# Attention in front of a soft mixture of experts: scores by single heads into two banks, masks added on TensorE, and a written order for four engines

## The chip, the cores and the metric

The kernel runs on one core of a Trainium2 chip. A core has engines that work side by side, each through its own queue in order: TensorE (PE, matrix products and transposes, into the eight banks of PSUM), VectorE (DVE), ScalarE (ACT), GpSimd (POOL, which here works on SBUF only) and SyncE (SP, which issues the transfers). The metric is the device time of one execution in microseconds; a lower time is better. The profile is of one execution; its times are microseconds from the start of its span.

## The reference

There are 8 batches, 8 heads of 64 columns, 512 local and 32 global tokens. A global query sees all 544 keys. A local query sees the 32 global keys and the local keys at a distance of at most 32. The output of the attention is the input `x` of a soft mixture of 8 experts with 4 slots each.

```python
s_ll = scale * np.matmul(q_l, k_l.transpose(0, 1, 3, 2))
mask = np.abs(pos[:, None] - pos[None, :]) <= window          # 32
s_ll = np.where(mask, s_ll, -1000000000.0)
a_l = sm(np.concatenate([s_lg, s_ll], axis=-1))
out_l = np.matmul(a_l, np.concatenate([v_g, v_l], axis=2))
...
logits = x @ phi                       # 4352 tokens, 32 slots
d = softmax(logits, over the tokens)   # dispatch
slot_input = d.T @ x
slot_out[e] = np.maximum(slot_input[e] @ w1[e], 0.0) @ w2[e]
return softmax(logits, over the slots) @ slot_out             # combine
```

## The kernel before

**Units.** A unit is one batch and four heads, two pairs; there are 16. The 512 local queries of a head are 16 blocks of 32. A block needs 128 keys: its own, the block before, the block after, and the global one. The host lays the keys out so that these 128 are contiguous or nearly so (the global block is repeated after every third block).

**Scores** (`scores`, line 159). The queries lie block-diagonally: two heads share 128 rows, and 64 columns of weights hold the block's 32 queries of either head, zeros elsewhere. One product gives 64 rows of scores over 128 keys, so a PSUM bank (128 rows by 512) holds four blocks of all four heads. A unit has four such banks (`kb`). The trace shows each fp32 product as two matmuls with their weight loads.

**Softmax.** DVE adds the masks to the bank (line 166), takes the maximum of each group of 128 (line 177) and subtracts it into SBUF, turning the order of the keys where needed (line 183). PE transposes the result (line 200), and ACT takes the exponential on the way out of the bank (line 204). `pv` (line 220) multiplies with the values, which carry a column of ones for the denominator; blocks use one of three forms of the values, the loaded one and two copies shifted by 32 rows that `make_v` writes: `va` on POOL (lines 143, 144), `vb` on ACT (lines 147, 148). DVE divides (lines 229 to 231).

**Global queries.** Products of 480 and 64 columns (lines 241, 246), two maxima on DVE (lines 249, 250), four shifts on ACT (line 259), five transposes (line 268), 20 products (line 278), four scaled copies on ACT (line 286).

**Dispatch** (`moe_steps`). When a batch is complete, its 512 tokens are transposed (`xt`, line 313, copied out on ACT at line 316), multiplied with `phi` (line 323), go through a running softmax over the tokens (lines 346 to 368), the weights are turned (`turn`, lines 382 to 391; `turn_logits` puts the logits into the same bank, line 397, copied on ACT at line 399), and the slots' sums are updated (line 406, added at line 413). The global tokens are dispatched in two halves of four batches.

**Experts.** After the attention come the first product (line 564), hidden layer, second product (line 738), and the combination (line 767). Weights come in 64 pages of 512 KB, of which 30 have room of their own and the others take buffers that the attention gives back.

**PSUM.** Three banks for scores (`psS`), two for transposes (`psT`), two for values (`psV`) and one for the dispatch (`psM`).

**Order.** In the attention a planner puts the instructions of each engine in order by its own costs. From the last unit's end on, PE follows an order written out by hand (`manual_schedule`), and within the last softmax DVE and ACT too. `pieces` cuts a batch's dispatch into five steps that are run between the banks of the next units.

## Time and profile before

| what | value |
|---|---|
| time, median of 3 (lowest to highest) | 324.7 us (324.51 to 325.45) |
| span of the profiled execution | 324.0 us |
| PE busy | 294.7 us, 91% |
| DVE busy | 220.3 us, 68% |
| ACT busy | 186.7 us, 58% |
| POOL busy | 48.6 us, 15% |
| moved by DMA | 76.26 MB, mean 235 GB/s |

The profiled execution has no time of its own beside its span; the span is 0.7 us under the median of the timed runs. In the rows, `L159` is line 159 of the kernel, `s<-k,qlo` says that a product writes tile `s` from `k` and `qlo`, and `x16` counts instructions. PEld is the loading of weights, which overlaps the products. A row of the chain of waits has the start, the time that the piece holds the chain, and what it is. A row of the groups has the busy time, the mean nanoseconds of one instruction, and the idle time ahead with what ended it.

### The profile page before, as it was taken

How to read it: one execution, taken by the hardware profiler on the slowest of the kernel's cores; microseconds unless marked ns; L12 is line 12 of the kernel's file. 1: busy time of each engine (PE TensorE's matmuls, PEld its weight loads, DVE VectorE, ACT ScalarE, POOL GpSimd, SP SyncE). 2: the span in 40 equal slices, each digit the busy share in tenths (PEclk: the TensorE clock that was granted, in tenths of full speed). 3: DMA queues.
4: the chain of work that ended last, by engine and by line, in shares of the span. 5: the costliest groups of instructions: out<-in, count | busy, mean ns of one | idle time of the engine just before them, and what ended most of it. 6: DMA issues, size and time to landing. Idle time of an engine off the chain costs nothing.

```text
span 324.0 us, 12624 instructions
## 1 busy us (share of the span) xinstructions
PE 294.7 (91%) x5277; PEld 217.9 (67%) x5277; DVE 220.3 (68%) x730; ACT 186.7 (58%) x538; POOL 48.6 (15%) x72
## 2 busy tenths in 40 slices
PE   6789999999999999999999999999999999999600
PEld 5677877777777877777678778777876433665500
DVE  1877868696788677875886786868785795244600
ACT  1368577586847675767476756848584320263600
POOL 2312212031111111111111120303110000000000
PEclk9999999999999999999999999999999999999955
DMA  6878787789968897755444535355548999967792
GB/s 193 258 251 246 259 269 280 239 261 293 315 231 270 284 324 246 230 170 160 137 106 160 171 87 173 96 171 149 156 165 293 405 393 406 409 238 271 239 351 61
DMA packets 30969, 76.26 MB, mean 235 GB/s; under 512 B 3136, under 2 KB 12352, under 8 KB 30912
## 3 DMA queue, kind: packets, MB, share of 16 engines
q1 hardware_dynamic: 30912, 75.45, 70.3%
q8 instruction: 42, 0.69, 0.9%
q14 instruction: 15, 0.12, 0.1%
HBM read 66.52 MB, written 8.91 MB: 233 GB/s over the span
## 4 chain that ended last, share of the span: by engine, by line
PE 81%; ACT 5%; DVE 4%; DMA 3%; issue 1%; SPq 1%; DVEq 0%; ACTq 0%
PE s L159 21%; PE o L220 11%; PE t L200 10%; PE xt L313 5%; PE po L738 5%; PE g L241 5%; PE ph L564 5%; PE tg L268 3%; PE pc L767 3%; PE pl L323 3%; PE pa L406 3%; PE og L278 2%; ACT xg L286 2%; DMA qhi<-in_qT_dram 2%; DMA v<-in_vS_dram 1%
## 5 line engine op out<-in xcount | busy, mean ns | idle before, releaser
L166 DVE TENSOR_TENSOR s<-s,con 128x64 f32<-128x64 f32 (+1 forms) x112 | 35.3, 315 | 43.5 <-PE s L159 30.2
L143 POOL COPY va<-v 128x650 f32<-128x650 f32 x32 | 23.4, 732 | 190.1 <-PE o L220 173.0
L159 PE MATMUL s<-k,qlo 128*64 128x128 f32 x512 | 47.4, 298 | 1.8 <-DMA qlo<-in_qT_dram 1.6
L183 DVE TENSOR_TENSOR sp<-s,mx 128x256 f32<-128x256 f32 (+5 forms) x128 | 48.2, 417 | 0.2
L159 PEld LDWEIGHTS s<-k,qlo 128*64 128x64 f32 x512 | 37.5, 204 | 11.3 <-issue 9.3
L220 PE MATMUL o<-v,pt 128*32 128x65 f32 x768 | 43.7, 223 | 1.5 <-ACT xg L286 1.4
L177 DVE TENSOR_REDUCE mx<-s 128x4 f32<-128x512 f32 x64 | 43.9, 687 | 0.9
L204 ACT ACTIVATE pt<-t 128x256 f32<-128x256 f32 x128 | 41.1, 383 | 4.9 <-PE t L200 4.7
L220 PE MATMUL o<-va,pt 128*32 128x65 f32 x768 | 42.2, 222 | 0.6
L147 ACT COPY vb<-v 64x260 f32<-64x260 f32 x62 | 25.2, 406 | 28.3 <-DMA v<-in_vS_dram 11.0
L159 PE MATMUL s<-k,qhi 128*64 128x128 f32 x512 | 39.4, 293 | 1.8 <-DMA qhi<-in_qT_dram 1.8
L220 PE MATMUL o<-vb,pt 128*32 128x65 f32 x512 | 40.9, 223 | 0.0
L200 PE MATMUL t<-con,sp 128*128 128x128 f32 x256 | 39.6, 284 | 0.3 <-ACT pt L204 0.2
L159 PEld LDWEIGHTS s<-k,qhi 128*64 128x64 f32 x512 | 32.9, 202 | 7.1 <-issue 6.0
L220 PEld LDWEIGHTS o<-v,pt 128*32 128x32 f32 x768 | 32.6, 110 | 6.7 <-ACT xg L286 2.8
L220 PEld LDWEIGHTS o<-va,pt 128*32 128x32 f32 x768 | 31.9, 110 | 3.9 <-PE og L278 1.2
L286 ACT ACTIVATE xg<-og,rg 32x64 f32<-32x64 f32 x64 | 19.5, 305 | 22.7 <-PE o L220 18.5
L200 PEld LDWEIGHTS t<-con,sp 128*128 128x128 f32 x256 | 27.3, 141 | 4.8 <-ACT pt L204 0.4
L220 PEld LDWEIGHTS o<-vb,pt 128*32 128x32 f32 x512 | 30.5, 110 | 0.0
L231 DVE TENSOR_TENSOR xh<-o,r 128x256 f32<-128x256 f32 x64 | 26.6, 416 | 0.8
L148 ACT COPY vb<-v 64x260 f32<-64x260 f32 x62 | 25.3, 408 | 0.8
L144 POOL COPY va<-v 32x650 f32<-32x650 f32 x32 | 23.0, 719 | 2.0
(150 smaller groups left out, 434.2 us busy)
## 6 DMA issues: line engine op xcount, KB each, us to landing
w<-in_w_dram SPq DMA_DIRECT2D x64, 512.0 KB, 6.8
v<-in_vS_dram SPq DMA_DIRECT2D x32, 390.0 KB, 3.9
k<-in_kT_dram SPq DMA_DIRECT2D x15, 672.0 KB, 6.6
out_dram<-ob SPq DMA_DIRECT2D x16, 512.0 KB, 5.2
qhi<-in_qT_dram SPq DMA_DIRECT2D x32, 144.0 KB, 3.7
qlo<-in_qT_dram SPq DMA_DIRECT2D x32, 128.0 KB, 3.6
k<-in_kT_dram SPq DMA_DIRECT2D x1, 512.0 KB, 4.2
out_dram<-ob SPq DMA_DIRECT2D x4, 128.0 KB
```

Source lines behind the costliest of these rows:

```text
L143: nc.gpsimd.tensor_copy(va, v[:, 0:5])
L147: copy(vb[64:128, m:m + 2], v[64:128, m:m + 2])
L148: copy(vb[0:64, m:m + 2], v[0:64, m + 1:m + 3])
L159: nc.tensor.matmul(ps[64 * pr:64 * pr + 64, i, :], q[:, :, q0 + i, pr], ks[u][:, pr, s0:s0 + P], start=True, stop=True)
L166: nc.vector.tensor_add(a, a, m)
L177: nc.vector.reduce_max(mx, ps, axis=AX.X)
L183: nc.vector.tensor_tensor(sp[:, t0:t1, b0:b0 + a1 - a0], ps[:, t0:t1, a0:a1], bc(mx[:, t0:t1], a1 - a0), ALU.subtract)
L200: tlast[0] = nc.tensor.transpose(pt[:, i, :], sp[:, i, :], ident)
L204: nc.scalar.activation(e, pt[:, :, 64 * pp:64 * pp + 64], AF.Exp, scale=SCALE)
L220: ins = nc.tensor.matmul(po[32 * cc:32 * cc + 32, t2, jj, :], pts[u, kb, pp][:, i, 32 * jj:32 * jj + 32], (vs, vas, vbs)[cls][u, pp][:, m, ...
L231: nc.vector.tensor_tensor(xhs[u][:, 2 * th:2 * th + 2, P * pp:P * pp + P].rearrange("p t (h d) -> p t h d", h=2), po[:, :, :, 0:D], bc(r, ...
L286: nc.scalar.mul(xg[p0:p0 + 32, 256 * g + D * j:256 * g + D * j + D], po[32 * j:32 * j + 32, 0:D], r[32 * j:32 * j + 32])
```

## The change

- **Half-units.** A unit is worked in two halves of eight blocks (`k` counts 32 of them). The eight blocks of four heads fill one tile of two banks.
- **Scores.** Queries are laid out plainly. One product takes the 64 rows of one head and 32 query columns, over 128 keys. The heads of a pair lie in the two row halves and write different banks; pair and block choose one of four column groups. A half-unit has 32 such products, 64 matmuls in a trace. Key windows are read through strided views, so that all blocks have the same order of keys and nothing is turned.
- **Masks.** A bf16 mask of a whole bank is multiplied with a bf16 identity into each bank ahead of the scores, which accumulate onto it. The constants bring the masks as a transfer of their own (`msk`), cast at the start.
- **Softmax.** One maximum and one shift over both banks on DVE, two banks of transposes, each with one exponential.
- **Values.** One tile of two banks per half-unit, one reciprocal, two multiplications. Both shifted copies of the values are made on POOL.
- **Global queries.** Products of 512, 32 and 96 columns into a two-bank tile, one maximum, one shift on ACT. Their value products and all of the dispatch use the two `psT` banks.
- **PSUM.** Two tiles of two banks for scores and global scores (`psA`), one of two for values (`psV`), two banks `psT`; the split of before comes back after the attention.
- **Loads.** Keys, queries and values of a unit come as one transfer each, with two buffers each.
- **Order.** PE, DVE, ACT and POOL follow the written order through the attention and up to the first product.

```diff
+PAIRS = [
+    [(0, 1), (4, 7), (3, 6), (2, 5)],
+    [(10, 13), (9, 12), (8, 11), (14, 15)],
+]
...
+    psV = p_ps.enter_context(tc.tile_pool(name="psV", bufs=1, space=PS))
+    psA = p_ps.enter_context(tc.tile_pool(name="psA", bufs=2, space=PS))
...
+    def make_v(k):
...
+        nc.gpsimd.tensor_copy(va, v[:, m0:m1])
+        nc.gpsimd.tensor_copy(va[0:32], v[0:32, m0 + 1:m1 + 1])
+        nc.gpsimd.tensor_copy(vb[64:128], v[64:128, m0:m0 + 2])
+        nc.gpsimd.tensor_copy(vb[0:64], v[0:64, m0 + 1:m0 + 3])
...
+    def masks(k):
+        ps = psA.tile([P, 2, 512], F32, tag="s", name=f"s{k}")
+        for hh in range(2):
+            nc.tensor.matmul(ps[:, hh, :], identb, maskb[:, k % 2, :], start=True, stop=False, skip_group_check=True)
+        pss[k] = ps
...
+    def scores(k):
+        u, a = k // 2, k % 2
+        for s, cs in enumerate(PAIRS[a]):
             for pr in range(2):
+                for j, c in enumerate(cs):
+                    g = 2 * pr + j
+                    for hh in range(2):
+                        nc.tensor.matmul(
+                            pss[k][32 * g:32 * g + 32, hh, P * s:P * s + P],
+                            qs[u][64 * hh:64 * hh + 64, pr, 32 * c:32 * c + 32], window(u, c, hh, pr),
+                            start=False, stop=True, skip_group_check=True)
+
+    def shift(k):
+        ps = pss.pop(k).rearrange("p h (s j) -> p (h s) j", j=P)
+        mx = xp.tile([P, 8], F32, tag="mx", name=f"mx{k}", bufs=2)
+        nc.vector.tensor_reduce(mx, ps, axis=AX.X, op=ALU.max, negate=True)
+        sps[k] = a2.tile([P, 8, P], F32, tag="sp", name=f"sp{k}", bufs=2)
+        nc.vector.tensor_tensor(sps[k], ps, bc(mx, P), ALU.add)
+
+    def transpose_exp(k):
...
+        for hh in range(2):
+            pt = psT.tile([P, 4, P], F32, tag="t", name=f"t{k}_{hh}")
+            for s in range(4):
+                nc.tensor.transpose(pt[:, s, :], sp[:, 4 * hh + s, :], ident)
+            nc.scalar.activation(e[:, hh], pt, AF.Exp, scale=SCALE)
...
+    def global_scores(u):
+        k = ks[u]
+        pg = psA.tile([P, 1024], F32, tag="s", name=f"g{u}")
+        for c0, n, src in ((0, 512, 32), (512, 32, 21 * 32), (544, 96, 17 * 32)):
+            for pr in range(2):
+                nc.tensor.matmul(pg[64 * pr:64 * pr + 64, c0:c0 + n], qg[:, pr, :], k[:, pr, src:src + n],
+                                 start=True, stop=True)
+        pgs[u] = pg
+
+    def global_shift(u):
+        pg = pgs.pop(u)[:, 0:640]
         m1 = xp.tile([P, 1], F32, tag="m1", name=f"m1_{u}")
+        nc.vector.tensor_reduce(m1, pg, axis=AX.X, op=ALU.max, negate=True)
+        nc.scalar.activation(spg, pg, AF.Identity, bias=m1)
...
         def turn():
             n = R.stop - R.start
-            ptl = psM.tile([P, 2, P], F32, tag="m", name=f"ptl{name}")
+            ptl = psT.tile([P, 2, P], F32, tag="t", name=f"ptl{name}")
...
+    order = tc.manual_schedule(engines={ENG.PE, ENG.DVE, ENG.Activation, ENG.Pool})
+    order.__enter__()
+    nc.vector.tensor_copy(identb, ident)
+    nc.vector.tensor_copy(maskb, mtmp)
+    make_qg(0)
+    masks(0)
+    scores(0)
+    shift(0)
...
+    def dispatch(b, srcs, name, k0):
...
+            steps.setdefault((k0, "c"), []).append(lambda: (xt(0), xt(1)))
+            steps.setdefault((k0 + 2, "c"), []).append(lambda: (xt(2), xt(3)))
+            k0 += 2
+        steps.setdefault((k0, "b"), []).append(logit)
+        steps.setdefault((k0 + 1, "c"), []).append(lambda: turn_logits(turn()))
+        steps.setdefault((k0 + 2, "b"), []).append(slots)
+
+    for b in range(B - 1):
+        dispatch(b, xlocal(b), str(b), 4 * b + 5)
+    dispatch(None, xglobal(0), "g0", NU + 5)
...
+    for k in range(NH):
+        u = k // 2
+        if k % 2 == 0 and k >= 2:
+            global_transpose(u - 1)
+        run(k, "c")
+        if k >= 1:
+            transpose_exp(k - 1)
+        if k + 1 < NH:
+            masks(k + 1)
+        if k >= 2:
+            values(k - 2)
+        if k % 2 == 0 and k >= 2:
+            global_values(u - 1)
+        run(k, "b")
+        if k + 1 < NH:
+            if k % 2 == 1:
+                make_qg(u + 1)
+            scores(k + 1)
+            shift(k + 1)
+        if k % 2 == 0:
             global_scores(u)
+            global_shift(u)
...
+        make_v(k)
...
-    order = tc.manual_schedule(engines={mybir.EngineType.PE})
-    order.__enter__()
...
+    global_transpose(NU - 1)
+    run(k, "c")
+    transpose_exp(k - 1)
+    values(k - 2)
+    global_values(NU - 1)
...
     xt(0)
     xt(1)
+    values(k - 1)
...
     st6["sums"](pa6[0], 0)
     st6["add"](pa6[0], slice(0, 256))
     logits(0)
     logits(1)
+    xtg(0)
     xt(2)
+    xt(3, True)
+    for hc in range(4):
+        logitsg(hc)
     logits(2)
     logits(3)
```

## The prediction

> **What bounds the kernel now.** I read the page's shares first, then the chain of waits in order of time, then the groups by line and form, then the stretches.

> ```profile
> PE 294.7 (91%) x5277; PEld 217.9 (67%) x5277; DVE 220.3 (68%) x730; ACT 186.7 (58%) x538; POOL 48.6 (15%) x72
> PE   6789999999999999999999999999999999999600
> PE 81%; ACT 5%; DVE 4%; DMA 3%; issue 1%; SPq 1%; DVEq 0%; ACTq 0%
> ```

> TensorE (PE) is busy nearly throughout and makes 81% of the chain that ends last. Matmul durations overlap, so I price PE by how long a run of one kind holds the chain, with its count:

> ```profile
> 40.10 0.59 PE t L200 x4
> 40.69 1.01 PE g L241 x4
> 41.70 0.17 PE g L246 x4
> 41.87 1.02 PE t L200 x8
> ...
> 45.75 0.66 PE s L159 x8
> 46.41 1.02 PE xt L313 x8
> 47.43 0.67 PE s L159 x6
> 48.10 0.71 PE og L278 x40
> ...
> 53.33 0.57 PE pl L323 x16
> 53.90 1.13 PE s L159 x16
> 55.03 0.60 PE o L220 x32
> ...
> 59.05 1.00 PE pa L406 x16
> ...
> 70.00 1.01 PE g L241 x4
> ...
> 223.41 1.01 PE g L241 x4
> ...
> 251.32 0.31 DVE top L343
> ```

> Comparing runs of 4 and 8 transposes: each costs (1.02-0.59)/4 = 0.109 us, plus about 0.15 per run, which is paid when the kind of matmul (its tile of the array) changes. So 128 fp32 columns through one full-width tile take 109 ns. Scores, two tiles side by side: (1.13-0.66)/8 = 0.058. Values, four tiles: (0.60-0.13)/32 = 0.0146 for 65 columns. Column tiles thus run in parallel. The global scores' g rows recur every 14.6 us per unit of four heads (40.69 to 70.00 is two units), and of that little is idle: attention is bound by PE. At 251.32 the last softmax begins; the rest, up to 324.0, is expert work that the change leaves as it is.

> **The change part by part.** The fixed order makes each engine go through its work as written. A batch is four half-units k (32 in all); in each PE does: transposes of k-1, masks of k+1, values of k-2, scores of k+1; even ones add global transposes, global values and, last, the global scores of the unit; a dispatch adds four xT transposes in two odd ones, logits, turn and slot sums. PE work of such a cycle, in us:

> - probability transposes 32 x 0.109 = 3.5, as before;
> - values 256 x 0.0146 = 3.7, as before (fewer, larger divisions follow);
> - global transposes 10 x 0.109 = 1.1 and values 2 x 0.58 = 1.2; xT 16 x 0.109 = 1.7; logits 32 x 0.029 = 0.9; turn 0.2; slot sums 0.9: all as before;
> - global scores: 640 instead of 544 columns, (1.01+0.17-0.15)/544 x 640 = 1.2, twice, 2.3;
> - scores: 256 instructions of 128 columns instead of 128. Eight tiles (two row halves, four column groups) take turns. The trace has no row halves. Bounds: 0.029 us each, as logits with four column tiles (0.57-0.11)/16, if row halves take turns; 0.0146, as values, if they overlap (half of 0.029, and the shortest spacing shown). The two halves read other partitions and write other banks, so I take 0.0146: 3.7, where 128 x 0.058 = 7.4 is removed;
> - masks: eight new bf16 matmuls of 512 columns. Bounds from the nearest rows:

> ```profile
> 1.19 3.70 PE L118 MATMUL pw<-wrm 128*128 128x256 bf16 x18 [1.19 <-DVE wrm L474]
> 284.73 0.67 PE pc L767 x4
> ```

> Eighteen of 256 bf16 columns in 3.7 at the start give 0.39 for 512, the fp32r products (0.67-0.15)/4 x 2 = 0.26. I take 0.26, from warm mid-kernel work: 2.1.

> Sum 21.4. Mode runs: four in an even half-unit, three in an odd, 14 x 0.15 = 2.1. PE work 23.5 a cycle, against 29.3 measured now; the fixed order also saves the many short runs (about 30 a cycle now).

> [...]

> What the other engines lose and gain:

> ```profile
> L177 DVE TENSOR_REDUCE mx<-s 128x4 f32<-128x512 f32 x64 | 43.9, 687 | 0.9
> L183 DVE TENSOR_TENSOR sp<-s,mx 128x512 f32<-128x512 f32 x16 | 11.0, 690 | 0.2
> L183 DVE TENSOR_TENSOR sp<-s,mx 128x128 f32<-128x128 f32 x16 | 4.5, 279 | 0.0
> L249 DVE TENSOR_REDUCE m<-g 128x1 f32<-128x480 f32 x16 | 10.3, 646 | 0.1
> L259 ACT ACTIVATE spg<-g,m 128x384 f32<-128x384 f32 x16 | 9.6, 600 | 0.1
> L316 ACT COPY xT<-xt 128x512 f32<-128x512 f32 x31 | 17.0, 589 | 6.6 <-PE xt L313 6.4
> L166 DVE TENSOR_TENSOR s<-s,con 128x64 f32<-128x64 f32 (+1 forms) x112 | 35.3, 315 | 43.5 <-PE s L159 30.2
> L147 ACT COPY vb<-v 64x260 f32<-64x260 f32 x62 | 25.2, 406 | 28.3 <-DMA v<-in_vS_dram 11.0 <-issue 8.3 <-PE o L220 6.6
> L143 POOL COPY va<-v 128x650 f32<-128x650 f32 x32 | 23.4, 732 | 190.1 <-PE o L220 173.0 <-DMA v<-in_vS_dram 17.1
> L397 PE MATMUL ptlg<-con,lTg 32*128 32x32 f32 x1 | 0.2, 245 | 0.3 <-DVE dg L391 0.3
> ```

> DVE loses the mask adds, 35.3; from 690 and 279 an element costs 1.07 ns over a fixed 0.14, so a two-bank maximum and a two-bank shift are 1.24 each, 2.5 a half-unit. ACT loses the vb copies (2 x 25), which go to POOL: about 2.7 a half-unit by 732 for 650, 85 in all, behind PE's other half-units and out of the way. The larger loads have two buffers and a half-unit or more of slack. What these savings relieve was not the bound, so I price them at nothing.

> What the order costs. I walk through the four lists: each instruction starts when the one ahead of it on its engine and its last input are done. Times run from PE's end of scores k+1 (0):

> - *Odd half-units with xT.* The global scores stand last in the even one. DVE starts the shift at 0.24 (pipeline 0.17 and signal), ends at 2.75; only then the global maximum of 640 (0.82): 3.5; ACT's one global shift (640 elements, 0.28+0.53 by the 600 ns form) runs 3.6 to 4.4. Behind it on ACT stand the two xT copies. PE ends the global scores at 1.3 and the eight xT transposes at 2.3; both transpose banks are then full, and the probability transposes need the first xT copy, 4.35 to 4.95, so PE waits from 2.3 to 5.0 (2.6 before rounding). Everything of the next score bank is queued behind. Two a cycle.
> - *Even half-unit with turn.* The second transpose of the turn waits for DVE's copy d, as the last row shows. That copy now stands behind the whole shift, and the shift behind the running softmax (which waits for ACT): it ends 3.4 after 0, while PE has 1.2 of work. With 0.2 and 0.15 of bank waits before it: 2.3 there.
> - Small bank waits with two transpose banks for everything: 1.0 a cycle.

> Cycle: 23.5 + 2 x 2.6 + 2.3 + 1.0 = 32.0, against 29.3. Half-units are 8.2 (odd), 6.5 or 9.1 (even).

> **Sum**, against the profiled execution (span 324.0; the median, 324.7, is 0.7 above it):

> - *Start to the third unit's global scores,* 40.69 now:

> ```profile
> 4.58 5.73 DMA qhi<-in_qT_dram
> 23.76 4.30 DMA v<-in_vS_dram
> 0.00:10.00 10.00, 5.85 (x50) 4.46 (x50) 3.29 (x8) 1.28 (x1) 1.89 (x7) 1.00 0.77 219
> ```

>   k, q, constants and masks are 1.92 MB; at 219 GB/s 8.8 us after 0.7 of issue, and 1.0 for the two casts (1024 elements) and signals: first mask at about 11. The same walk over half-units 0 to 4, which have no dispatch, gives 25.2. 36.2, so -4.5; both waits above end inside it.
> - *Six cycles, 40.69 to 223.41,* 182.7 now: 6 x 32.0 + 3.8 for the dispatch of the first global half, with a turn wait of its own, = 195.5 (by half-units unrounded). +12.8.
> - *From there to the last softmax,* 27.9 now. Global scores 1.3, three half-units (8.2, 6.5, and 6.4 without masks and scores), then the written tail: PE work 9.3, and waits 5.7 (1.9 in the turn, 1.6 until ACT's four global copies free a bank, 1.2 until DVE has divided the last values, the rest small), 15.1: 37.5. +9.6.

> 324.0 - 4.5 + 12.8 + 9.6 + 0.7 = 342.6.

> **Rivals.**

> *The row halves take turns* (the change doesn't do what it says): scores 0.029 each, 0.93 more a half-unit, of which the waits swallow a little: +25, 368. For it: no row shows row tiles. Against it: column tiles overlap fully. [...]

> *Faster: the waits aren't there.* Place: ACT's and DVE's queues. If xT copies pass the global shift and d passes the shift, or the work is planned apart from the text as in the attention now, 15 waits of 2.6 and 8 of 2.3 go, 57 in all: 285 at full, 314 at half. It decides from 18 saved, i.e. 0.8 off each of the 23. For it: PE work falls by 5.8 a cycle, and now the same transposes and copies rarely stall. Against it: one queue per engine, the order given for all four, and the d wait stands in a row.

> *Loads late*: q and k come as whole tiles; if units 1 and 2 each wait once more as at 23.76, +9, 352.

> **How the numbers follow.** Forecast 0.50 (own range 331 to 353: 0.4 a wait either way and start +-2); row halves in turn 0.15; waits gone, in part or whole, 0.30; loads late 0.05. Under 0.3% (1 us) is what this measurement can't tell from no change. Faster is 0.27 of the third case, same 0.03, slower the rest, 0.70. The range goes from 302, which leaves out the deeper half of the third case, to 368.

> **What would show it.** PE waits of over 2 us before probability transposes in odd half-units, ended by the ACT copy of xT; one of about 2 before the second turn transpose, ended by DVE d; score runs of 64 at about 1.1 us (2.0 if halves take turns); mask matmuls at 0.22 to 0.39. Wrong if the global scores recur every 14 us or less per unit.

## The result, and the profile after

The changed kernel takes 380.44 us (median of 4 runs, 377.95 to 382.9), the kernel before 325.07 beside it: ratio 1.170, 95% interval 1.164 to 1.176. It is slower, as forecast, but by 55 us where 18 were forecast, and it lies outside the range (302 to 368). The profiled execution has a span of 380.8 us. Three of the kernels further down also had runs in a slower state; their times and ratios are of the faster runs alone.

First the page of the kernel after: the busy time of the engines, TensorE (PE) in 40 slices, the granted clock in the same slices, and the queue that brings instructions.

```profile
PE 282.1 (74%) x6398; PEld 198.7 (52%) x6429; DVE 177.9 (47%) x390; ACT 128.9 (34%) x296; POOL 94.5 (25%) x167
PE   4887587777877977766777777977796789999800
PEclk9999898889888989998896888988899899999965
q8 instruction: 50, 0.82, 0.9%
```

Every engine but POOL has less to do than before (PE 294.7, DVE 220.3, ACT 186.7), and PE is idle for a quarter of the span, where it was idle for a tenth. Two things in these lines stood in no step of the prediction: the clock is cut during attention, and PE has 12,827 recorded instructions (before 10,554), which come in 50 blocks of 16 KB (before 42).

PE's longest waits in the kernel after (what waits, for what: us in total, times, longest):

```profile
PE t L205 <- ACT xT L310: 28.4, 13, 2.4
PE ptl L390 <- DVE d L384: 12.3, 7, 2.4
PE s L187 <- issue: 7.2, 5, 3.6
PE o L224 <- issue: 5.3, 11, 1.3
...
PE og L268 <- issue: 2.9, 2, 1.9
PE xtg L302 <- ACT xT L310: 2.4, 1, 2.4
```

The first two rows are the two waits of the forecast, at their places and up to 2.4 us long (forecast 2.6 and 2.3). The three "issue" rows, 15.4 us, are time in which PE waits for nothing that the profile shows; the kernel before has one such row among its waits:

```profile
PE tg L268 <- issue: 0.9, 1, 0.9
```

The timeline around one odd half-unit with xT shows the first wait at work, and its sequel:

```profile
114.46 1.36 PE L243 MATMUL g<-k,qg 128*64 128x512 f32 x12
114.59 1.22 DVE L195 TENSOR_REDUCE mx<-s 128x8 f32<-128x1024 f32 x1
115.75 1.09 PE L308 MATMUL xt<-con,xh 128*128 128x128 f32 x8
115.84 1.22 DVE L197 TENSOR_TENSOR sp<-s,mx 128x1024 f32<-128x1024 f32 x1
116.99 0.81 DVE L250 TENSOR_REDUCE m<-g 128x1 f32<-128x640 f32 x1
117.89 0.79 ACT L251 ACTIVATE spg<-g,m 128x640 f32<-128x640 f32 x1 [2.08 <-DVE m L250]
118.58 1.06 ACT L310 COPY xT<-xt 128x512 f32<-128x512 f32 x2
119.22 1.97 PE L205 MATMUL t<-con,sp 128*128 128x128 f32 x8 [2.37 <-ACT xT L310]
```

The shift, the global maximum, the global shift and the xT copies run one behind the other, and eight transposes wait 2.37 us for them. Then these eight take 1.97 us, though eight of the same width took 1.09 at 115.75. The windows of 1 us over the same stretch say why (the number behind POOL's is the granted clock):

```profile
117.00:118.00 1.00, 0.00 (x0) 0.00 (x0) 0.80 (x2) 0.11 (x1) 0.00 (x0) 1.00 0.73 239
...
119.00:120.00 1.00, 0.78 (x4) 0.79 (x5) 0.00 (x0) 0.65 (x2) 0.00 (x0) 0.50 0.46 183
```

Shortly before the wait ends, at 118.90, the clock drops to half. In the trace's record of the clock there are 18 such stretches that start between 40 and 300 us, 17 of 3.41 us and one of 6.83, 65 us in all. Here a gap of 2.37 us went ahead of the drop.

The six cycles of the kernel before and then the three stages of the kernel after, as windows:

```profile
41.00:223.00 182.00, 180.02 (x3544) 139.82 (x3541) 138.74 (x473) 124.12 (x373) 34.08 (x48) 1.00 0.66 210
```

```profile
0.00:42.00 42.00, 29.19 (x749) 19.99 (x756) 18.63 (x31) 11.25 (x23) 15.69 (x32) 0.98 0.90 335
42.00:267.00 225.00, 170.15 (x4372) 127.23 (x4398) 108.36 (x222) 80.12 (x189) 69.24 (x120) 0.87 0.46 158
267.00:307.00 40.00, 30.73 (x738) 22.84 (x738) 17.91 (x43) 16.30 (x39) 9.53 (x16) 0.91 0.47 149
```

The six cycles take 224.9 us (global scores start at 41.93 and at 266.85), where 195.5 were forecast and 182.7 were taken before. PE has 10 us less busy time there than before, although about a quarter of the stage ran at half the clock: the mean is 0.87.

### The profile page after: what moved, and what is told of

The parts are those of the page before. It is cut to its first block, busy times and chain, and to the rows that moved or that the text cites. A ratio compares the mean times of both kernels' runs of the same rounds, so it can differ in the third digit from the quotient of the medians.

```text
span 380.8 us, 14224 instructions
## 1 busy us (share of the span) xinstructions
PE 282.1 (74%) x6398; PEld 198.7 (52%) x6429; DVE 177.9 (47%) x390; ACT 128.9 (34%) x296; POOL 94.5 (25%) x167
## 5 line engine op out<-in xcount | busy, mean ns | idle before, releaser
L205 PE MATMUL t<-con,sp 128*128 128x128 f32 x256 | 44.1, 324 | 30.1 <-ACT xT L310 28.4
L151 POOL COPY va<-v 128x520 f32<-128x520 f32 (+1 forms) x32 | 23.2, 725 | 167.9 <-PE o L224 154.5
L195 DVE TENSOR_REDUCE mx<-s 128x8 f32<-128x1024 f32 x32 | 39.1, 1222 | 18.3 <-PE s L187 17.5
L187 PE MATMUL s<-k,q 64*32 64x128 f32 x2048 | 40.9, 281 | 7.4 <-issue 7.2
L224 PE MATMUL o<-vb,pt 128*32 128x65 f32 x512 | 43.9, 250 | 0.9 <-issue 0.9
L206 ACT ACTIVATE pt<-t 128x512 f32<-128x512 f32 x64 | 36.2, 596 | 15.0 <-PE t L205 14.8
L197 DVE TENSOR_TENSOR sp<-s,mx 128x1024 f32<-128x1024 f32 x32 | 39.2, 1224 | 1.1
L187 PEld LDWEIGHTS s<-k,q 64*32 64x32 f32 x2048 | 30.2, 108 | 16.4 <-issue 14.8
L274 ACT ACTIVATE xg<-og,rg 32x64 f32<-32x64 f32 x64 | 19.6, 306 | 48.6 <-DVE rg L272 38.1
L243 PE MATMUL g<-k,qg 128*64 128x512 f32 (+2 forms) x192 | 23.8, 386 | 0.5 <-DVE sp L197 0.5
L260 ACT ACTIVATE ptg<-tg 128x256 f32<-128x256 f32 (+1 forms) x32 | 13.5, 436 | 30.2 <-PE tg L258 29.9
L152 POOL COPY va<-v 32x520 f32<-32x520 f32 (+1 forms) x32 | 23.1, 720 | 2.0
L168 PE MATMUL s<-maskb,identb 128*128 128x512 bf16 x33 | 16.8, 514 | 5.9 <-DVE maskb L474 3.6
```

Of the source, the lines that this page charges most:

```text
L151: nc.gpsimd.tensor_copy(va, v[:, m0:m1])
L152: nc.gpsimd.tensor_copy(va[0:32], v[0:32, m0 + 1:m1 + 1])
L168: nc.tensor.matmul(ps[:, hh, :], identb, maskb[:, k % 2, :], start=True, stop=False, skip_group_check=True)
L187: nc.tensor.matmul(pss[k][32 * g:32 * g + 32, hh, P * s:P * s + P], qs[u][64 * hh:64 * hh + 64, pr, 32 * c:32 * c + 32], window(u, c, hh, pr),
L195: nc.vector.tensor_reduce(mx, ps, axis=AX.X, op=ALU.max, negate=True)
L197: nc.vector.tensor_tensor(sps[k], ps, bc(mx, P), ALU.add)
```

## The experiments

Three explanations were on the table. By theory A of the texts below the two waits cost time and so does the clock that drops with them, by theory B the waits alone do, and by theory C it is PE's many small matmuls and how their instructions are supplied. The first four runs share their runs of the kernel before (324.92).

**The global shift later.** It goes behind the next half-unit's transposes, so that ACT reaches the xT copies first.

```diff
         if k >= 1:
             transpose_exp(k - 1)
+        if k % 2 == 1:
+            global_shift(u)
...
             global_scores(u)
-            global_shift(u)
```

> The global maximum and the global shift are written behind the next half-unit's probability transposes, so ACT's two xT copies no longer stand behind them; nothing else is changed. Theory A (the two queue waits carry the loss, and each also lets the TensorE clock fall to half afterwards): the 13 waits of 2.4 us go and most half-clock stretches with them, 380 - 31 - 14 = 335 (328 to 345). Theory B (waits alone, the half clock costs nothing of its own): 349. Theory C (PE's many small matmuls and their supply are what costs; the waits would reappear elsewhere): above 370.

**The turn later.** Both transposes of the turn go behind the masks, and the second takes a bank of its own.

```diff
-        steps.setdefault((k0 + 1, "c"), []).append(lambda: turn_logits(turn()))
+        steps.setdefault((k0 + 1, "m"), []).append(lambda: (turn(), turn_logits()))
...
             masks(k + 1)
+        run(k, "m")
```

> The turn is written behind the masks of the same half-unit, and its two transposes get a bank each, so PE no longer waits for DVE's copy d behind the shift. Theory A: 7 waits of 2.4 us and the clock stretches that follow them go, 380 - 17 - 3 = 360 (352 to 367). Theory B: 363. Theory C: above 372.

**Both.**

> Both moves together. Theory A: no wait over 1.5 us is left in the steady part, the clock stays at 1.00 there, 312 (300 to 325). Theory B: 332. Theory C: above 355.

Measured: 345.92 us with the shift later (ratio 1.064, 1.060 to 1.068), 361.29 with the turn later (1.112, 1.107 to 1.117), 331.14 with both (1.018, 1.014 to 1.022). PE's waits, with the shift later, with the turn later, and with both:

```profile
PE ptl L390 <- DVE d L384: 11.4, 7, 2.3
...
PE t L205 <- ACT xT L310: 3.1, 13, 0.2
```

```profile
PE t L205 <- ACT xT L310: 28.6, 13, 2.4
```

```profile
PE s L187 <- issue: 13.4, 7, 3.4
PE og L268 <- issue: 5.2, 3, 2.4
...
PE t L205 <- ACT xT L310: 3.1, 13, 0.2
...
PE xt L308 <- issue: 2.1, 1, 2.1
```

Each edit takes away just its own wait. But 25.3 us of wait (28.4 - 3.1), and 2.2 of the same kind at xtg, gave 34.5 us of time, and both together (25.3 + 12.3 = 37.6, and 4.3 at xtg and ptlg) gave 49.3. The surplus is clock: stretches at half clock fell from 65 us to 17, and PE's busy time for the same instructions from 282.1 to 262.3, by 19.8. Against that, the waits for nothing visible grew from 15.4 to 20.7. By their times alone the two kernels with the shift later lie nearer to theory B (349 and 332) than to A (335 and 312): the clock costs less than A had it. In the kernel with both edits eight transposes take 1.14 at full clock:

```profile
107.45 1.14 PE L205 MATMUL t<-con,sp 128*128 128x128 f32 x8 [0.24 <-ACT xT L310]
108.43 0.38 PE L168 MATMUL s<-maskb,identb 128*128 128x512 bf16 x1
108.95 0.24 PE L224 MATMUL o<-va,pt 128*32 128x65 f32 x1
...
116.02 1.16 PE L187 MATMUL s<-k,q 64*32 64x128 f32 x64
```

**The waits filled.** The changed kernel in its own order, with 20 matmuls of 256 columns into a bank that nobody reads in each xT wait and each turn wait: the waits stay, PE is kept busy.

```diff
         run(k, "c")
+        if k % 2 == 1 and (k, "c") in steps:
+            warm(NFILL, psV, "v")
...
+            if fill:
+                warm(NFILL, psV, "v")
             nc.tensor.transpose(ptl[:, 1, 0:n], st["lT"][R, :], ident[R, R])
```

> The order stays as in the changed kernel; 20 bf16 matmuls of 256 columns into a free bank, about 2.1 us, are written into each of the waits of 2.4 us. They compute nothing that is used. Theory A: the waits stay, the granted clock stays near 1.00, and the time at half clock is won back: 380 - 27 = 353 (346 to 362). Theory B: 380, the clock is a symptom. Theory C: longer than 380, 800 instructions more.

Measured: 370.82 us (1.140, 1.138 to 1.143), 9.6 below the changed kernel and between theory A (353) and theory B (380); the time at half clock fell from 65 us to 27. Timeline of this kernel, then its waits:

```profile
104.75 2.35 PE L126 MATMUL pw<-maskb 128*128 128x256 bf16 x20
107.31 1.14 PE L206 MATMUL t<-con,sp 128*128 128x128 f32 x8 [0.22 <-ACT xT L311]
```

```profile
PE s L188 <- issue: 9.6, 5, 4.2
PE g L244 <- issue: 4.2, 1, 4.2
```

The transposes behind the filled wait take 1.14 again, not 1.97. So the clock drops because of the waits, and it costs time by itself. 37.5 us less at half clock are worth up to 19; 9.6 came out. The filling takes part of that back: here 2.56 us lie between the start of the filling and the next transposes, where the wait was 2.37. The two issue rows shown make 13.8, so the waits for nothing visible didn't shrink.

**The loads in order.** The kernel with both edits and the changed kernel, each with SP's loads as written, so that a page of expert weights starts in every half-unit and not all that fit at once. The idea was that bursts of these pages hold up something PE needs.

```diff
-    order = tc.manual_schedule(engines={ENG.PE, ENG.DVE, ENG.Activation, ENG.Pool})
+    order = tc.manual_schedule(engines={ENG.PE, ENG.DVE, ENG.Activation, ENG.Pool, ENG.SP})
```

> Both moves, and SyncE's queue follows the written order too: one weight page per half-unit instead of bursts of five or six pages that the planner puts between the loads of keys, queries and values. Instructions, tiles and bytes are the same. Theory D (PE's waits for which the profile shows no releaser, 21 us with both moves, 17 in the changed kernel, 1 before, are waits for blocks of instructions that lie behind such bursts): these waits fall below 8 us, 331 - 13 = 316 (311 to 321). Rival E (PE is out of instructions because 64 products and their weight loads run faster than instructions can be brought, whatever else moves): the waits stay, 331 (329 to 334).

> The changed kernel with SyncE's queue in the written order, nothing else. Theory D: the 17 us of waits without a releaser fall below 6, the queue waits for ACT and DVE stay, 380 - 11 = 369 (364 to 374). Rival E: 380 (376 to 383).

Measured: 332.57 us with both edits (1.022, 1.015 to 1.028), no gain, and 383.12 in the changed kernel (1.179, 1.172 to 1.185), none either. With both edits the waits stay:

```profile
PE s L187 <- issue: 17.3, 9, 3.1
```

The bursts of weight pages are not the cause.

**The list moved.** I then counted PE's recorded instructions (weight loads, matmuls and waits on semaphores, in order of time) up to each stop of over 0.7 us for nothing visible in the kernel with both edits. The stops stand some 255 or a multiple of it apart, whatever the work at that place, and 12,900 instructions in 50 blocks make 258 a block. The test puts 128 instructions ahead of everything, in the idle time before the first load, and leaves the rest as it is.

```diff
     warm(NWARM)
+    for _ in range(64):
+        nc.tensor.matmul(pw[:, 0:32], wrm[:, 0:P], wrm[:, 0:32], start=True, stop=True)
```

> The kernel with both waits moved (331.1 us), with 64 matmuls of 32 columns more behind the warm-up matmuls, that is 128 instructions more at the head of TensorE's list, half a block; they run while TensorE waits for the first load. Nothing else is changed. Theory F (blocks of instructions): every one of these waits moves by 128 instructions towards the head of the list: none is left within the run of scores at which each stood (43 of the 64 matmuls of a run done at the wait of 3.4 us), and they stand elsewhere, with a sum that can be larger or smaller by some us (325 to 335 us). Rival G (the dense run of small matmuls itself stalls TensorE, for instance a queue that it fills): the waits stay at the same matmuls of the same runs, and the time is 331 within 1.

Measured: 336.19 us, a single run. The number of the recorded instruction at each larger stop, and its remainder by 256 (the trace of the kernel with both edits misses 31 matmuls, 6398 of 6429, which is why its remainder drifts; the others miss none; the last row is of a kernel further down):

```
both edits    702 1468 2234 2489 2744 3510 4021 5808 6574 7340 9893   remainder 190 188 186 185 184 182 181 176 174 172 165
list moved    705  961 1985 2241 3009 3777 4545 10433 11201  remainder 193 each time
values split  705 1217 1473 2241 2497 3009 3265 4033 5057 5825 6849 9921  remainder 193 each time
```

```profile
PE s L187 <- issue: 19.1, 9, 3.9
```

The program moved by half a block, and the stops did not move with it: the one of 3.4 us that stood within a run of scores at 1468 would be at about 1,600 now, and there is none. What stops PE is the edge of a block of instructions, not the work at that place.

**Without the loads.** Both edits, and from the third unit on no keys, queries and values are loaded.

```diff
     def load_k(u):
+        if u >= 2:
+            ks[u] = ks[u - 2]
+            return
```

> The kernel with both waits moved (331.1 us), with the loads of keys, queries and values of units 2 to 15 left out: from unit 2 on it computes on the data of units 0 and 1 again, so its output is another. In the kernel with both waits moved, TensorE's waits for nothing that the profile shows sit at its recorded instructions 702, 1468, 2234, 2489, 2744, 3510, 4021, 5808, 6574 and so on: steps of 255 or a multiple of it, in which a block of 16 KB of instructions is used up. Theory F: TensorE runs dry because a block of instructions (256) is asked for late and the dense stretch ahead of it is used up in about 2 us, faster than a block comes. If the blocks come late because the data transfers fill the DMA engines (F1), the waits fall from about 20 us to under 6 and the time to 312 to 318. If they are late whatever the traffic (F2), 15 us or more of them stay and the time is 326 to 333.

Measured: 318.19 us, a single run. The stage from 55 to 235 us, as a window (the last numbers are the granted clock, the DMA share and GB/s) and PE's waits in it, of the kernel with both edits and then of the one without loads:

```profile
55.00:235.00 180.00, 152.89 (x4377) 113.37 (x4401) 107.79 (x222) 81.34 (x191) 69.74 (x119) 0.97 0.55 187
...
PE s L187 <- issue: 10.0, 6, 2.7
PE og L268 <- issue: 3.7, 2, 2.4
...
PE xt L308 <- issue: 2.1, 1, 2.1
```

```profile
55.00:235.00 180.00, 163.91 (x4778) 120.00 (x4768) 116.27 (x246) 90.02 (x214) 75.45 (x129) 1.00 0.06 18
...
PE s L196 <- issue: 3.4, 4, 1.4
```

With 18 GB/s in place of 187, 15.8 us of stops become 3.4. Over the whole kernel 11.0 are left of 20.9 (under 6 were expected), most of them ahead of 55 us, where weight pages still load (387 GB/s between 20 and 55 us). The trace also has the transfers of the instruction blocks (queue q8, which the page counts among the same 16 DMA engines as the data). Each takes 0.9 to 1.7 us, with loads or without. With the list moved and with the values split, each of the 21 stops listed above ends 1.2 to 1.7 us after a block has landed, and no block is entered sooner than 1.2 us after it. What the loads change is when the transfer starts: between 55 and 235 us that is up to 4.1 us after PE has entered the block ahead (values split), without loads at most 2.0. So the blocks come late while the loads run (a mean DMA share of 0.55 in this stage, 0.06 without them). By the starts of the recorded instructions, from the entry into a block to the entry into the next the four stops left in this stage show 3.2 to 3.7 us; with loads there are up to 7.7 (15.23 to 22.89, in the kernel with the list moved). At its densest the list after uses up 256 instructions in 1.9 us; the list before never took less than 3.7 for 256 in its attention, which fits that it has next to no such stops.

**The value products split.** Half of a half-unit's value products go behind the next scores, with banks of their own, so that the densest stretch thins out.

```diff
-            values(k - 2)
+            values(k - 2, (0,))
...
+        if k >= 2:
+            values(k - 2, (1,))
         make_v(k)
```

> The kernel with both waits moved (331.1 us), with the value products of a half-unit split: the first half (32 matmuls, 64 instructions) where it stood, the second half behind the scores of the next half-unit and the global scores, each half with a bank of its own and its own three VectorE operations behind it (two small ones more per half-unit, about 0.35 us of VectorE). The densest stretch of TensorE's list, some 330 instructions in 2.5 to 3.5 us from the value products to the last score, loses 64 of them. Theory F: a block then lasts over 3 us nearly everywhere, the waits fall from 20 us to 5 to 10, half-clock stretches with them, and the time falls to 314 to 322. Rival G or a loss at the new bank waits: 329 to 336.

Measured: 327.3 us (1.004, 1.0004 to 1.0075), where the kernel with both edits had 1.018. Both are set against the kernel before, so the split gains some 1.4%, but not in the way expected:

```profile
PE o L224 <- issue: 8.8, 4, 3.3
PE s L187 <- issue: 8.4, 7, 2.0
```

With three smaller rows the stops still make 20.0 us (expected 5 to 10). Their edges fall on other work, but while the loads run, 2.5 to 5.4 us of work still use up a block before the next has come. What fell is the time at half clock, from 17 us to 7.

**The row halves.** Are two heads' scores computed at once because neighbours in the list use different row halves? One kernel has the four upper scores of each group of eight ahead of the four lower ones, another has all 32 upper ones of a half-unit ahead of the lower 32; the diff is of the latter.

```diff
+        for hh in range(2):
...
             for pr in range(2):
                 for j, c in enumerate(cs):
                     g = 2 * pr + j
-                    for hh in range(2):
```

> Both moves, and within each group of eight scores all of the upper row half are written ahead of all of the lower, instead of taking turns; the same products into the same places. If row halves overlap because neighbours in the queue lie in different halves, four column groups are left and a run of 64 takes 0.15 + 64 x 0.029 = 2.0 us instead of 1.1, about 25 us more in all. If the spacing is set by issue alone, nothing changes.

> The kernel with both waits moved (331.1 us), with the row half as the outermost loop of the scores: all 32 matmuls of the upper heads of a half-unit, then all 32 of the lower ones. If two matmuls run at once only because neighbours in the list use different row halves, a run of 64 takes 2.0 to 2.3 us in place of 1.16, which is 32 x 1.0 = 32 us: 355 to 365 us. If what spaces them is something else (each start 17 ns behind the last, whatever the row half), a run stays at 1.16 and the time at 329 to 333.

Measured, in a single run each: 326.43 us with groups of four, a run of 64 still 1.16; 342.08 with the half outermost:

```profile
119.47 1.56 PE L187 MATMUL s<-k,q 64*32 64x128 f32 x64
```

Against the kernel with both edits (331.14) that is +11, and 32 x (1.56 - 1.16) = 12.8. So mixing the halves does help, and four in a row of one half cost nothing yet. With one matmul's 0.27 us taken off, the starts are (1.56 - 0.27)/63 = 0.0205 us apart within one half and (1.16 - 0.27)/63 = 0.0141 with the halves mixed. Neither expectation for the outermost loop was met: it costs something, but a third of what was expected of halves that run strictly in turn.

To see whether the 326.43 meant a better order, it was joined to the split values.

> The kernel with split value products (327.3 us, 0.4% behind the kernel before) with the order of the scores of the look at 326.43 us (the four upper scores of a group ahead of its four lower ones). If the 4.7 us by which that look was below the kernel with both waits moved belong to the order of the scores, the time is 321 to 324 and the ratio 0.985 to 0.997. If they were chance, since a run of 64 took 1.16 us in both, the time is 326 to 329 and the waits for blocks of instructions stay at 18 to 21 us at the same steps of 256.

Measured: 329.22 us (1.013, 1.010 to 1.017). So this order gains nothing there, and 326.43 stays a single run. No version that loads all its data is faster than the kernel before; the best is level with it within half a per cent.

## Why the prediction was wrong, point by point

- **Direction and the two waits: right.** "What the order costs" named both waits, their places and releasers. Thirteen xT waits of 2.2 on average (forecast 2.6), the turn waits 1.8 (2.3). PE's waits of the kernel after in the six cycles:

```profile
PE t L205 <- ACT xT L310: 23.7, 11, 2.4
PE ptl L390 <- DVE d L384: 12.0, 6, 2.4
PE o L224 <- issue: 3.7, 9, 0.9
PE s L187 <- issue: 3.5, 4, 0.9
```

  With xtg (2.4) and the turn of the global half (2.1), the two kinds make 40.2, where the forecast had 6 x 7.5 and 3.8 with the first global half, about 49.
- **Prices of the new work: right.** Scores 0.0146 each, 64 in 1.1 us: 0.0141, 1.16. VectorE's two-bank operations 1.24: 1.22. Global maximum 0.82: 0.81; ACT's global shift 0.81: 0.79. Masks 0.26: from the first mask at 108.43 to the value products a pair takes 0.52, with 0.15 for the change of kind taken off (0.52 - 0.15)/2 = 0.19 each; the 20 matmuls of the filling, with one matmul's 0.27 taken off, give (2.35 - 0.27)/19 = 0.11 for 256 columns, 0.22 for 512. So nearer to 0.19 to 0.22. No row of the kernel before shows the 0.22 of "mask matmuls at 0.22 to 0.39"; 0.19 to 0.22 is what these runs show.
- **"Cycle: 23.5 + 2 x 2.6 + 2.3 + 1.0 = 32.0" is the step that failed.** It prices a wait at its length, and has PE at full clock and never short of instructions. What a cycle takes without any of that shows in the kernel without loads, which has both edits and the same products:

```profile
70.04:96.12 26.08, 24.56 (x736) 18.04 (x732) 17.80 (x36) 13.22 (x31) 11.63 (x21) 1.00 0.02 4
```

  The next cycle there takes 25.95 (96.12 to 122.07). That is 26.0 where 23.5 + 1.0 was forecast (29.3 before). Of the 224.9 us, 6 x 26.0 = 156 are work at full clock, some 4 the dispatch of the first global half, 40 the waits, 9 waits for nothing visible (3.7 + 3.5, and 1.9 at og); 15 are left for the clock. PE's busy time agrees: it is 170.1 in these cycles and 152.4 in those without loads (43.37 to 207.08), 17.7 less. The granted clock took 225 x (1 - 0.87) = 29 at most, part of it while PE stood idle. So the 29.4 us that the forecast missed in this stage are some 15 to 18 of clock, 9 for the supply of instructions and 13 of work priced too low, less 9 for waits forecast too long. That the clock costs time by itself is shown by the filled waits; its share is worked out, not measured alone.
- **"Start ... 36.2": wrong, 41.93.** The first mask came at 8.86, before the 11 forecast. Then three stops at block edges, each of which ends 1.2 to 1.5 us after a block has landed (at 22.66, 29.24 and 39.68):

```profile
24.14 0.31 PE L268 MATMUL og<-v,ptg 128*32 128x65 f32 x5 [1.00 <-issue]
30.69 0.25 PE L224 MATMUL o<-va,pt 128*32 128x65 f32 x2 [1.26 <-issue]
40.93 1.06 PE L187 MATMUL s<-k,q 64*32 64x128 f32 x20 [3.61 <-issue]
```

  Together 5.9, where the stage is 5.7 over the forecast; since the first mask was 2.1 early, some 2 us stay unexplained.
- **"37.5" to the last softmax: nearly right.** 266.85 to 306.34 is 39.5, and a clock of 0.91 over 40 us accounts for up to 3.6.
- **The larger loads, priced at nothing: wrong in effect.** None of PE's longer waits is for q, k or v, but without these loads the kernel with both edits is 13 us faster (318.19), with 11.0 us of stops for instructions in place of 20.9. "Fewer, larger" and smaller instructions were counted by their durations alone; no step of the prediction asked how fast the list itself is supplied.
- **The rivals.** Row halves in turn: no, though one half alone is slower (1.56 us for 64 scores against 1.16). Waits gone: they were there, and the 285 us given for it were wrong too. With both waits really gone it is 331, with 20.7 us of stops and 17 at half clock still in it. Loads late: not as waits for data.

## What to carry to other kernels

A wait of TensorE that repeats can cost more than its length, because the clock falls with it: here 27.5 us of waits gave 34.5 us of time, and half clock, for 3.41 us in 17 of the 18 stretches of the kernel after, followed 80 of the 88 times when TensorE was idle for over half of a step of 3.41 us (the grid of the next section). Allow for that, or put work into the wait. Splitting matmuls into more and smaller ones adds instructions: count how fast the list is used up at its densest, and compare it with what the kernel before got by with (here 1.9 us for 256 instructions against 3.7), above all where loads run (15.8 us of stops at 187 GB/s, 3.4 at 18). And where all engines follow a written order, look for the short copy that stands behind a long operation: moving two such steps won back 49 of the 55 us.

## What the runs showed of the hardware beyond that

Stops for instructions stand 193 instructions into each 256 recorded ones, in the kernels whose traces miss no record, whatever work is there. Their length goes with the data traffic: at most 1.4 us at 18 GB/s (without loads, 55 to 235 us), up to 4.2 us among loads (with the waits filled).
